# A weight ring with four slots instead of five, one more chunk kept resident, and value rows stored group by group

## The chip, the core and the metric

The kernel runs on one core of a Trainium2 chip. The metric is device microseconds (us) of one execution. Three runs of the kernel before took 1798.37, 1800.26 and 1802.88 us; the median is 1800.26 us.

## What is computed

The program computes two independent parts from the reference and writes them side by side.

```python
a = _A_ref(q, k, v, shift_k, ssm_k, ssm_D)   # short filter over k, times v, long convolution by FFT, times q
for s in range(n_seg):                        # B: 64 segments of 32 tokens, each behind the one before
    h = concatenate([mem, x[s]])              # 8 memory rows and 32 tokens, 1024 wide
    q, k, v = h @ Wq, h @ Wk, h @ Wv          # 32 heads of 128
    p = softmax(mask(q @ k.T * scale))
    o = (p @ v) @ Wo                          # 4096 -> 1024
    mem = o[:8]                               # memory of the next segment
    outs.append(o[8:])
return concatenate([a, b], axis=-1)
```

Part B is a recurrence: segment s+1 needs the first eight output rows of segment s. Its four weights hold 64 chunks of 128x2048 bf16 (512 KB each, 32 MB in all), more than fits on the chip, and all 64 are needed in every segment.

## The kernel before

**Stages.** Part A (L53 to L420) runs first, with dense work for part B filled into it: the keys and queries of 8 of each segment's 32 tokens (`dense`, L618) go to the DRAM tensor `REC`, and their value rows (L756 to L770) to `VBD`. After that the loop over segments (L920) holds all that is serial. In it the token matrix of 32 columns (8 memory rows and 24 tokens) goes through the projections in `Proj` (L933), and the 8 other tokens join from `REC` and `VBD`.

**Chunks.** `ORDER` (L26) lists the 64 chunks in the order of use in a segment as (matrix, chunk, group): 0 to 7 K and 8 to 15 Q in a mixed order, both of group 0 up to place 15; 16 to 23 K and 24 to 31 Q of group 1; 32 to 39 V of group 0 and 40 to 47 V of group 1; 48 to 63 the output weights, in the order `O_ORDER`. `STREAM` (L29) names the places that are not resident. There are 16; the two places 56 and 57 are loaded in segment 0 only and then kept in PSUM (`keep`, L821), so 14 chunks are streamed in each later segment: places 0, 6, 13, 19, 24, 29, 35, 40, 45, 51, 52, 54, 58 and 63. Of place 52 (`PART`) a quarter is resident, so its load has 384 KB. The other 48 chunks are resident, in tiles Wmid, Wres, Wmore, Wlate, pw and Wring.

**The ring.** Streamed chunks are first copied to the DRAM tensor `WS`. `fetch` (L715) takes the next chunk of the list `loads` and the slot that came free first, and issues the load on SyncE's queue (SP). `done` (L862) runs after the last matmul of a chunk: it gives its slot back and calls `fetch` once. With five slots (`free = [4, 5, 0, 1, 3]`, L708), a load is thus issued when the streamed chunk five places ahead of it in the stream has been used, and it has from then until its own use to land. Nothing else moves a load ahead. SP issues in program order, so an issue that waits holds up those behind it. The order of the matmuls is written out by hand (L1055 to L1125); a scheduler orders the work only ahead of the loop.

**Output weights.** In the loop the chunk at place 51 (output pair 3) is used in both column halves one after the other, ahead of the second attention; places 52 to 55 come next, then 58, and place 63 (pair 14) is the last of `LAST` in the first column half and the first in the second (L1115).

**GpSimd's queue (POOL)** issues in each segment, in this order: the two output stores (L1127), the load of the value rows `VBs` (L925), two copies into KT (L929), and the load of the next segment's token matrix `rec` from `REC` (192 KB, L882), which waits for the last V matmul.

**Slots that become resident.** Slots wring2 and wring3 serve as staging tiles (`pair`, `X_sb`, `xt`) ahead of the loop. In segment 0, wring3 becomes the fifth ring slot, and wring2 takes a resident chunk (L869) once the sixth streamed chunk is done. `late` lists the resident chunks that are loaded last; `place_late` takes them from its head.

**Value rows.** `VBD` has the layout [segment, token, c, i, (group, 128)]. The store of one group (L768) writes rows of 256 bytes, and the load of a segment (L925) reads both groups as rows of 512 bytes in one DMA.

Of the kernel before, what the change touches and what calls it, by code (L numbers as in the profile page):

```python
# [9 lines left out]
BF = mybir.dt.bfloat16  # L10
# [15 lines left out]
ORDER = [(0, kc, 0) for kc in (0, 1, 4, 5)] + [(1, kc, 0) for kc in (0, 1)] + [(0, kc, 0) for kc in (2, 3, 6, 7)] + \  # L26
    [(1, kc, 0) for kc in range(2, 8)] + [(m, kc, 1) for m in (0, 1) for kc in range(8)] + \
    [(2, kc, g) for g in range(2) for kc in range(8)] + [(3, hp, 0) for hp in O_ORDER]
STREAM = (0, 6, 13, 19, 24, 29, 35, 40, 45, 51, 52, 54, 56, 57, 58, 63)  # L29
N2, N3 = 12, 19  # L30
WO_COPY = 29
Q_LOAD = (10, 13, 16, 19)
X_LOAD = 1
STAGE3 = 34
LATE_RING = 5
RING = 5

PITCH = 2048
SCRATCH = 1024
# [383 lines left out]
def b_kernel(ctx: ExitStack, tc, x, mem0, Wq, Wk, Wv, Wo, outb, n_seg, run_a):  # L423
    nc = tc.nc
# [12 lines left out]
    streamed = set()  # L437
    for i in STREAM:
        streamed.add(order[i])
# [6 lines left out]
    late = [ch for ch in resident if ch not in placed]  # L446
# [15 lines left out]
    dram = ctx.enter_context(tc.tile_pool(name="b_dram", bufs=1, space=DRAM))  # L462

    REC = dram.tile([128, n_seg, 768], BF, name="REC")
    VBD = dram.tile([n_seg, 8, 4, 4, 256], BF, name="VBD")
    WS = dram.tile([len(ring_order), 128, PITCH], BF, name="WS")
    res = {}

# [10 lines left out]
    base = ctx.enter_context(tc.tile_pool(name="b0_base", bufs=1, side="right", reuse_waits="tile"))  # L479
# [3 lines left out]
    def xbt(kc):  # L483
        return XBT[kc // 4][:, kc % 4]
# [3 lines left out]
    def pair():  # L488
        turns["pair"] ^= 1
        return base.tile([128, 2048], BF, tag=f"wring{2 + turns['pair']}", name="pair")  # L490

    def slot16(shape, dt, name):
        turns["stage"] ^= 1
        return base.tile(shape, dt, tag=f"stage{turns['stage']}", name=name)
# [3 lines left out]
    def pw(k=None):  # L498
        if k is None:
            k = pw_next[0] % 8  # L500
            pw_next[0] += 1
        return pring.tile([128, 2048], BF, tag=f"pw{k}", name="pw")
# [63 lines left out]
    def group(m, g, temps={}, which=range(8), ws=None, eng=nc.sync, held=False):  # L566
        ws = ws or [None] * 8
        for kc in which:
            ch = (m, kc, g)
            if ch in res:  # L570
                got.append(eng.dma_start(res[ch], dram_chunk(ch)))
                ws[kc] = res[ch]
            else:
                t = temps[ch]() if ch in temps else pw()
                got.append(eng.dma_start(t[:], dram_chunk(ch)))
                if ch in streamed:
                    copies.append((stream_src(ch), t[:]))
                ws[kc] = t[:]
        while copies and not held:
            copied.append(nc.gpsimd.dma_start(*copies.pop(0)))  # L580
        return ws
# [28 lines left out]
    def evac(dst, src):  # L610
        flip[0] += 1
        if flip[0] % 3 and units[0] < STAGE3:
            nc.scalar.copy(dst, src)
        else:
            nc.vector.tensor_copy(dst, src)
# [35 lines left out]
    def store():  # L651
        if stores:
            nc.scalar.dma_start(*stores.pop(0))
# [40 lines left out]
    def more(i):  # L694
        return wres3.tile([128, 2048], BF, tag=f"Wmore{i}", name="Wmore")
# [5 lines left out]
    order_s = [ch for ch in order if ch in streamed]  # L701
    kept = {KEPT_A: "A", KEPT_B: "B"}
    at_hand = {}
# [1 line left out]
             if s == 0 and ch not in v_temp[2:] or s > 0 and ch not in kept]  # L705
    live = {}
    now = [0]
    free = [4, 5, 0, 1, 3]  # L708

    def slot():  # L710
        k = free.pop(0)
# [3 lines left out]
    def fetch():  # L715
        if loads:
            s, ch = loads.pop(0)
            live[s, ch] = k, t = slot()
            if ch in kept:
                nc.sync.dma_start(dst_view(t[:], ch), dram_chunk(ch))  # L720
            elif ch == PART:
                nc.sync.dma_start(t[:, 512:2048], stream_src(ch)[:, 512:2048])
            else:
                nc.sync.dma_start(t[:], stream_src(ch))

    def place(ch, ap):
        res[ch] = ap
        nc.sync.dma_start(dst_view(ap, ch), dram_chunk(ch))

    def place_late(n, tile_of):  # L730
        chs = [late.pop(0) for _ in range(n)]
        t = tile_of()
        for i, ch in enumerate(chs):
            place(ch, t[:, 2048 * i:2048 * i + 2048])
# [4 lines left out]
    with c0p:  # L739
        temps = dict(zip(v_temp, homes_v))  # L740
        wv = [group(2, 0, temps), None]
        for _ in rest:
            store()
        wv[1] = group(2, 1, temps)
        for i, ch in enumerate(v_temp):
            if i >= 2:
                home = (lambda i=i: more(i)) if i < len(v_temp) - 2 else (lambda k=i - len(v_temp) + 4: pw(k))
                at_hand[ch] = (wv[ch[2]][ch[1]], home)
        while stores:
            store()  # L750
        with tc.issue_after(got[-1].ins):
            for _ in range(2):
                fetch()
        n_k = len(own[0, 0])
        late = late[n_k:-2] + late[4:n_k] + late[:4] + late[-2:]
        for g in range(2):  # L756
            ws = wv[g]
            if g == 0:
                vsts = slot16([128, 4, 4, 512], BF, "vst")
            for tb in range(4):  # L760
                vst = vsts[:, tb] if g == 0 else pair()[:].rearrange("p (c w) -> p c w", c=4)
                for c in range(4):
                    ps = ps0.tile([128, 512], F32, tag="ps0", name="vb_ps")
                    for kc in range(8):
                        v_last = nc.tensor.matmul(ps[:], lhsT=xbt(kc)[:, 16 * tb:16 * tb + 16, :].rearrange("p s t -> p (s t)"),  # L765
                                                  rhs=ws[kc][:, c * 512:(c + 1) * 512], start=(kc == 0), stop=(kc == 7))
                    evac(vst[:, c, :], ps[:])
                nc.scalar.dma_start(  # L768
                    VBD[16 * tb:16 * tb + 16, :, :, :, g * 128:(g + 1) * 128].rearrange("s t c i e -> (s t) (c i) e"),
                    vst.rearrange("p c (i e) -> p (c i) e", i=4))  # L770
            if g == 0:
                with tc.issue_after(got[-1].ins):
                    place_late(4, stage_home)
                    for i in [*range(len(v_temp) - 2, n_more), *range(len(v_temp) - 2)]:
                        place_late(1, lambda: more(i))
                    place_late(1, lambda: pw(2))
                    place_late(4, stage_home)
        assert len(late) == len(at_hand) + 1

    one = ctx.enter_context(tc.tile_pool(name="b_one", bufs=1, side="right", reuse_waits="tile"))  # L780
    two = ctx.enter_context(tc.tile_pool(name="b_two", bufs=2, side="right", reuse_waits="tile"))
# [39 lines left out]
    def keep(ch):  # L821
        t = live[0, ch][1]
        if kept[ch] == "A":
            w = t[:].bitcast(I32).rearrange("p (hh dh f x) -> p hh f dh x", hh=2, dh=2, f=2)
            for q in range(4):
                bits(OTi[:, q, 160:416].rearrange("p (dh x) -> p dh x", dh=2), w[:, q // 2, q % 2])
        else:
            w = t[:].bitcast(I32)
            for q in range(4):
                for home, at in B_homes[q]:  # L830
                    n = home.shape[1] * (home.shape[2] if len(home.shape) == 3 else 1)
                    if len(home.shape) == 3 and n > 128:
                        for dh, o in enumerate(quarter_cols(q)):
                            bits(home[:, 2 * dh:2 * dh + 2, :], w[:, o // 2:o // 2 + 128].rearrange("p (b x) -> p b x", b=2))
                        continue
                    for dh, o in enumerate(quarter_cols(q)):
                        lo, hi = max(at, 128 * dh), min(at + n, 128 * dh + 128)
                        if lo < hi:
                            src = w[:, o // 2 + lo - 128 * dh:o // 2 + hi - 128 * dh]
                            bits(home if len(home.shape) == 3 else home[:, lo - at:hi - at], like(src, home))  # L840
# [21 lines left out]
    def done(ch):  # L862
        if now[0] == 0 and ch in at_hand:
            place_late(1, at_hand[ch][1])
        elif ch in streamed and (now[0] == 0 or ch not in kept):
            if now[0] == 0 and ch in kept:
                keep(ch)
            free.append(live.pop((now[0], ch))[0])
            if now[0] == 0 and ch == order_s[LATE_RING]:  # L869
                place_late(1, lambda: base.tile([128, 2048], BF, tag="wring2", name="Wring"))  # L870
            fetch()

    part = one.tile([128, 512], BF, name="part")
# [28 lines left out]
    with tc.manual_schedule():  # L902
        for _ in range(RING - 2):
            fetch()
# [15 lines left out]
        for s in range(n_seg):  # L920
# [1 line left out]
            last = s + 1 == n_seg  # L922
            hT, KBs, QBs = pend.pop(s)
            VBs = one.tile([128, 2, 128], BF, tag="VBs", name="VBs")
            nc.gpsimd.dma_start(VBs[:].rearrange("p g e -> p (g e)"), VBD[s].rearrange("t c i w -> (c i) t w"))  # L925

            def keys(g):
                KT = one.tile([128, 4, 4, 40], BF, tag="KT", name="KT")
# [271 lines left out]
```

## Time and profile before

| | |
|---|---|
| median of three runs | 1800.26 us |
| profiled execution, its own time | 1800.37 us |
| its span, first to last instruction | 1798.6 us |
| mean granted TensorE clock | 0.982 |
| first matmul of segment 0 / 1 / 63 | 440.33 / 471.52 / 1773.14 us |
| TensorE (PE) busy in 471.5 to 1791.5 us | 1297.27 of 1320 us |
| DMA share in the same stretch | 0.98, at 361 GB/s |
| DMA share in 364 to 438.7 us (value rows) | 0.99, at 307 GB/s |

Times in rows are us from the start of the span. In a timeline row the first number is the start, the second the duration of the whole row; several like instructions are merged ("x8"), and the bracket tells how long the engine sat idle before and who released it. A DMA has its issue on a queue ("SPq", "POOLq") and a landing, when its last byte has arrived; "to landing" counts from the start of the issue.

### The profile page before, as it was taken

The numbers are of one execution on the slowest core, as the hardware profiler recorded it, in microseconds if no ns is written. First come the engines' busy times: TensorE is split into PE (matmuls) and PEld (weight loads), VectorE is DVE, ScalarE is ACT, GpSimd is POOL, SyncE is SP. The second block draws the span as 40 slices with busy tenths as digits, with TensorE's granted clock in tenths as the row PEclk, the third lists the DMA queues.
The fourth block names the chain that finished last, engine by engine and source line by source line (L and its number), as shares of the span: only waits on it lengthen the run. The fifth ranks groups of instructions, "written<-read, shape, count | busy, mean of one in ns | idle before, by whom it ended". The sixth has DMA issues, their size and how long they took to land.

```text
span 1798.6 us, 70857 instructions
## 1 busy us (share of the span) xinstructions
PE 1690.5 (94%) x30744; PEld 995.1 (55%) x30776; DVE 1037.2 (58%) x3429; ACT 658.8 (37%) x1157; POOL 265.7 (15%) x499
## 2 busy tenths in 40 slices
PE   6988997697899999999999999999999999999998
PEld 2443323243566666666666666666666666666665
DVE  9926875432455555555555555555555555656555
ACT  6954651000233333333333333333333333333333
POOL 4102341100111111111111111111111111111111
PEclk9989998899899999999999999999999999999999
DMA  9989987999999999999999999999999999999998
GB/s 342 365 315 288 311 280 256 328 309 307 330 369 362 365 358 354 354 362 374 357 359 356 364 357 356 368 359 371 361 361 359 363 358 367 374 361 361 363 362 298
DMA packets 233069, 623.31 MB, mean 347 GB/s; under 512 B 72802, under 2 KB 72946, under 8 KB 232756
## 3 DMA queue, kind: packets, MB, share of 16 engines
q1 hardware_dynamic: 160948, 550.58, 82.8%
q0 software_dynamic: 17056, 45.13, 7.2%
q10 hardware_dynamic: 54752, 23.07, 4.8%
q8 instruction: 241, 3.95, 0.9%
q14 instruction: 72, 0.59, 0.1%
HBM read 563.63 MB, written 57.67 MB: 345 GB/s over the span
## 4 chain that ended last, share of the span: by engine, by line
PE 73%; DMA 13%; DVE 6%; ACT 5%; issue 3%; ACTq 1%; POOL 0%; SPq 0%; POOLq 0%; DVEq 0%
PE acc L945 32%; PE yacc L1036 21%; DMA wring<-WS 8%; PE kb_ps L624 5%; PE vb_ps L765 2%; PE tps L964 2%; ACT OT L1026 2%; PE tps L887 2%; DVE E L981 1%; DVE mx L979 1%; ACT s_sb L249 1%; DMA REC<-stage 1%; PE s_ps L247 1%; DMA VBD<-pair 1%; PE ks_ps L285 1%
## 5 line engine op out<-in xcount | busy, mean ns | idle before, releaser
L1036 PEld LDWEIGHTS <-OT 128*64 128x64 bf16 x8255 | 441.3, 110 | 52.8 <-ACT OT L1026 37.0
L945 PEld LDWEIGHTS <-rec 128*32 128x32 bf16 x12288 | 287.3, 96 | 277.2 <-DVE rec L898 41.2
L954 ACT CAST qkv_sb<-acc 128x512 bf16<-128x512 f32 x384 | 224.7, 585 | 519.1 <-PE acc L945 513.5
L945 PE MATMUL acc<-Wres,rec 128*32 128x512 bf16 x3328 | 239.5, 381 | 1.0 <-issue 0.9
L945 PE MATMUL acc<-wring,rec 128*32 128x512 bf16 x2300 | 227.9, 381 | 11.0 <-DMA wring<-WS 8.9
L1036 PE MATMUL yacc<-Wmore,OT 128*64 128x256 bf16 (+1 forms) x2560 | 221.2, 275 | 0.1
L945 PE MATMUL acc<-Wmid,rec 128*32 128x512 bf16 x3072 | 211.4, 379 | 0.9 <-issue 0.9
L1036 PE MATMUL yacc<-wring,OT 128*64 128x256 bf16 x2448 | 197.0, 274 | 6.2 <-DMA wring<-WS 3.2
L945 PE MATMUL acc<-pw,rec 128*32 128x512 bf16 x1796 | 144.4, 380 | 2.3 <-issue 2.2
L797 DVE TENSOR_SCALAR quarter<-OTp 128x256 int32<-128x256 int32 x252 | 99.5, 415 | 76.3 <-ACT OT L1026 76.3
L1125 ACT CAST Y<-yacc 128x256 bf16<-128x256 f32 x128 | 47.6, 372 | 257.8 <-DVE quarter_b L797 171.0
L1026 ACT CAST OT<-OTp 128x640 bf16<-128x640 f32 x128 | 87.4, 683 | 139.5 <-PE OTp L1018 139.4
L1127 POOL DMA_DIRECT2D out_dram<-Y x128 | 63.6, 502 | 485.0 <-ACT Y L1125 484.9
L945 PE MATMUL acc<-Wlate,rec 128*32 128x512 bf16 x1536 | 116.5, 379 | 0.0
L1064 DVE COPY KT<-tps 128x512 bf16<-128x512 bf16 x64 | 27.2, 425 | 153.8 <-PE tps L887 153.8
L898 DVE CAST rec<-tps 128x32 bf16<-128x32 f32 x128 | 24.5, 191 | 157.6 <-PE tps L896 153.6
L979 DVE TENSOR_REDUCE mx<-SB 128x8 f32<-128x320 f32 x128 | 62.9, 491 | 72.7 <-PE SB L973 72.7
L882 POOL DMA_DIRECT2D rec<-REC x64 | 36.2, 566 | 449.8 <-PE acc L945 433.7
L984 ACT ACTIVATE E<-E 128x320 f32<-128x320 f32 x128 | 60.1, 469 | 77.4 <-DVE E L981 77.3
L1036 PE MATMUL yacc<-Wlate,OT 128*64 128x256 bf16 x1024 | 78.9, 276 | 5.7
L624 PE MATMUL kb_ps<-XBT,pw 128*128 128x512 bf16 x314 | 81.6, 398 | 2.2 <-DMA pw<-in_B_Wk_dram 1.1
L929 POOL COPY KT<-rec 128x128 bf16<-128x128 bf16 x128 | 38.2, 299 | 263.2 <-PE SB L973 258.8
(222 smaller groups left out, 2630.6 us busy)
## 6 DMA issues: line engine op xcount, KB each, us to landing
wring<-WS SPq DMA_DIRECT2D x831, 512.0 KB, 6.1
wring<-WS SPq DMA_DIRECT2D x64, 384.0 KB, 5.4
rec<-REC POOLq DMA_DIRECT2D x64, 192.0 KB, 5.6
SK<-s_sb SPq DMA_DIRECT2D x16, 512.0 KB, 5.7
SU<-s_sb SPq DMA_DIRECT2D x16, 512.0 KB, 5.7
Kg<-SK SPq DMA_DIRECT2D x32, 256.0 KB, 4.3
Ug<-SU SPq DMA_DIRECT2D x32, 256.0 KB, 5.8
REC<-stage ACTq DMA_DIRECT2D x16, 512.0 KB, 13.0
```

The source lines that it names most:

```text
L624: nc.tensor.matmul(ps[:], lhsT=ws[kc][:, hl * 128:(hl + 1) * 128], rhs=xbt(kc).rearrange("p s t -> p (s t)"), start=(kc == 0), stop=(kc == 7))
L797: nc.vector.tensor_scalar(out=dst, in0=src, scalar1=0, scalar2=None, op0=ALU.bitwise_or)
L882: nc.gpsimd.dma_start(rec[:], REC[:, s, :])
L929: nc.gpsimd.tensor_copy(KT[:, :, :, 32:40], KBs[:, 128 * g:128 * g + 128].rearrange("p (c i t) -> p i c t", c=4, i=4))
L945: nc.tensor.matmul(self.acc[32 * c:32 * c + 32, :], lhsT=hT[:, ch[1], :], rhs=w[:, 512 * c:512 * c + 512], start=(ch == chs[0]), stop=(ch ...
L954: nc.scalar.copy(sb[:], self.acc[:])
L979: nc.vector.tensor_reduce(out=mx[:], in_=S, op=ALU.max, axis=AX.X)
L984: nc.scalar.activation(E[:], E[:], ACT.Exp, scale=scale)
L1026: nc.scalar.copy(OT[:], o_view)
L1036: nc.tensor.matmul(yacc[f][64 * dh:64 * dh + m, x - o:y - o], lhsT=lhsT, rhs=r, start=(h == (0, 2 * FIRST[-1])[f] and x == o), stop=stop, ...
L1125: nc.scalar.copy(Y[:, 256 * f:256 * f + 256], yacc[f][:, 0:256])
L1127: nc.gpsimd.dma_start(bass.AP(outb.tensor, outb.offset + SEG * s * 2048 + 512 * dh, [[2048, 32], [1, 512]]), Y[64 * dh + NM:64 * dh + 40, :])
```

## The change

```diff
-STREAM = (0, 6, 13, 19, 24, 29, 35, 40, 45, 51, 52, 54, 56, 57, 58, 63)
+STREAM = (0, 6, 13, 19, 26, 32, 38, 44, 51, 52, 55, 56, 57, 58, 63)
...
-LATE_RING = 5
-RING = 5
+LATE_RING = (5, 6)
+RING = 4
...
-    VBD = dram.tile([n_seg, 8, 4, 4, 256], BF, name="VBD")
+    VBD = dram.tile([2, n_seg, 8, 16, 128], BF, name="VBD")
...
-    free = [4, 5, 0, 1, 3]
+    free = [4, 5, 0, 1]
...
-        late = late[n_k:-2] + late[4:n_k] + late[:4] + late[-2:]
+        late = late[n_k:-3] + late[4:n_k] + late[:4] + late[-3:]
...
                 nc.scalar.dma_start(
-                    VBD[16 * tb:16 * tb + 16, :, :, :, g * 128:(g + 1) * 128].rearrange("s t c i e -> (s t) (c i) e"),
-                    vst.rearrange("p c (i e) -> p (c i) e", i=4))
+                    VBD[g, 16 * tb:16 * tb + 16].rearrange("s t h e -> (s t) (h e)"), vst.rearrange("p c w -> p (c w)"))
...
-            if now[0] == 0 and ch == order_s[LATE_RING]:
-                place_late(1, lambda: base.tile([128, 2048], BF, tag="wring2", name="Wring"))
+            if now[0] == 0 and ch in (order_s[i] for i in LATE_RING):
+                k = 2 + (ch == order_s[LATE_RING[1]])
+                place_late(1, lambda: base.tile([128, 2048], BF, tag=f"wring{k}", name="Wring"))
...
-            nc.gpsimd.dma_start(VBs[:].rearrange("p g e -> p (g e)"), VBD[s].rearrange("t c i w -> (c i) t w"))
+            for g in range(2):
+                nc.gpsimd.dma_start(VBs[:, g, :], VBD[g, s].rearrange("t h e -> h t e"))
```

Slot wring3 leaves the ring and takes a resident chunk in segment 0, as wring2 does, after the seventh streamed chunk. The ring has four slots, 49 chunks are resident, and a segment streams 13: places 0, 6, 13, 19, 26, 32, 38, 44, 51, 52, 55, 58 and 63. In `VBD` the two groups lie apart: a store writes one row of 4096 bytes for each partition, and a segment's value rows come in two DMAs with rows of 256 bytes.

More of the change, by code (lines that the diff above doesn't have):

```diff
@@ L777, in b_kernel @@
                     place_late(4, stage_home)
-        assert len(late) == len(at_hand) + 1
+        assert len(late) == len(at_hand) + 2
     one = ctx.enter_context(tc.tile_pool(name="b_one", bufs=1, side="right", reuse_waits="tile"))
```

## The prediction

> **What bounds the kernel now.** I read the stages first (busy times by stretch), then the chain that ended last, then single segments in the timeline, then the landings of single loads.
>
> The loop over segments takes 471.5 to 1791.5 us of a span of 1798.6. By stretch, value-row stage first, then the loop:
>
> ```profile
> 364.00:438.70 74.70, 62.37 (x277) 27.70 (x280) 24.00 (x35) 0.00 (x0) 4.10 (x8) 0.95 0.99 307
> 471.50:1791.50 1320.00, 1297.27 (x28490) 824.72 (x28490) 752.14 (x2830) 474.92 (x881) 168.70 (x377) 1.00 0.98 361
> ```
>
> The first figure after the stretch's length is PE busy, the last two are DMA share and GB/s. In the loop PE is busy 98% and the DMA engines 98%: both are nearly full. In the value-row stage PE is not (62.37 of 74.70 us), the DMA engines are.
>
> In the chain, in order of time, some segments are pure PE:
>
> ```profile
> 1518.25 4.49 PE yacc L1036 x80
> ...
> 1538.78 4.49 PE yacc L1036 x80
> ...
> 1559.31 4.49 PE yacc L1036 x80
> ```
>
> From one such row to the next is 20.53 us: the length of a segment in which nothing is waited for. The mean is (1773.14 - 471.52) / 62 = 20.99 us, from the starts of segments 1 and 63. So 0.46 us a segment, 29 us in 63 segments, is all that better loading could take from the loop. The waits tell what part of it is loads:
>
> ```profile
> PE acc L945 <- DMA wring<-WS: 8.9, 20, 1.1
> PE acc L945 <- issue: 4.5, 12, 0.9
> ```
>
> Ahead of the loop, two stalls come from the stores of value rows, as DVE waits for a staging tile whose store has not landed (7.03 + 2.20 us):
>
> ```profile
> 424.69 0.59 PE L765 MATMUL vb_ps<-pw,XBT 128*128 128x512 bf16 x1 [7.03 <-DVE pair L615]
> 435.25 0.38 PE L765 MATMUL vb_ps<-pw,XBT 128*128 128x512 bf16 x1 [2.20 <-DVE pair L615]
> ```
>
> **The change part by part.**
>
> *Value-row stores.* Eight stores of 512 KB change from 256-byte rows to 4096-byte rows. Now and beside it a ring load of the same size in 4096-byte rows:
>
> ```profile
> wring<-WS SPq DMA_DIRECT2D x831, 512.0 KB, 6.1
> VBD<-vst ACTq DMA_DIRECT2D x4, 512.0 KB, 15.1
> VBD<-pair ACTq DMA_DIRECT2D x4, 512.0 KB, 9.7
> ```
>
> The last number is us to landing. At 6.1 us a staging tile is free before its next use, two token blocks on (32 matmuls of 0.219 us, 7 us each), so both stalls go: 9.2 us. What is late next there is nothing that I see: the DMA engines fall idle after 434 us. The ends are 0 (another wait takes over) and 16 us; I take 9.2.
>
> *Segment 0* lasts 31.19 us (440.33 to 471.52), 10.7 over the floor, from loads that queue at its output weights. It gets one more resident load, two ring loads less in flight, and four streamed output chunks in a row (places 55 to 58). One load no longer waits on SP until the last value matmul (pw, issued at 437.39; its tile will be free a group earlier). I take 3 us gained, between -3 and 7.
>
> *Ahead of that* a copy to `WS` goes, and the scheduler shuffles some matmuls of part A's last stage with equal counts; 0, within 3 us either way.
>
> *Value-row loads.* POOL issues one more DMA of 0.53 us a segment (row VBs<-VBD). Behind it stands the first KT copy, now at 1210.95 us in one segment, whose reader starts at 1214.91: 3.4 us of cover are left. The second group lands about 1.93 + 1.07 + 5.6 us into the segment (issue and landing of today's rows); its readers come at 11.4 us: hidden. If that cover were gone, each us costs 63.
>
> *One chunk less, one slot less.* Traffic falls by 0.52 MB of some 7.5 MB a segment, 7%. That would ease the 0.46 us. But with four slots a load is issued after the use of the chunk four places ahead, not five. I took a segment without waits (start 1209.04) and read when each place is used. Rows of it:
>
> ```profile
> 1222.67 0.60 PE L1036 MATMUL yacc<-wring,OT 128*64 128x256 bf16 x8
> ...
> 1227.76 0.60 PE L1036 MATMUL yacc<-wring,OT 128*64 128x256 bf16 x8
> ```
>
> These are place 51 and place 63; SP issues the load after place 51 at 1223.31. The new places start, into the segment, at 0, 1.41, 2.93, 4.50, 6.48 (26), 8.21 (32), 9.94 (38), 11.80 (44), 13.63 (51), 14.72 (52), 16.43 (55), 17.09 (58) and 18.73 (63), next segment 20.53. An issue starts 0.44 us after a K, Q or V chunk starts and 0.64 after an output chunk. From issue to need, four places on, this leaves, in us: 4.85 for place 58, **4.46 for place 63**, 5.2 and 4.9 for the next segment's first two, 5.7 or more for all others. Today, with five slots, the shortest is 6.1.
>
> Place 63's load is issued at 14.27. Today a load is issued at that very point, for the next segment's place 0, and the trace tells how long it takes (three segments without waits, one of them the one above):
>
> ```profile
> L724 SPq DMA_DIRECT2D wring<-WS x1: 320/320/320, 1223.3 to 1223.3; - x1
> ...
> DMA to landing us min/median/max: 5.9/5.9/5.9
> ```
> ```profile
> L724 SPq DMA_DIRECT2D wring<-WS x1: 320/320/320, 1537.4 to 1537.4; - x1
> ...
> DMA to landing us min/median/max: 5.3/5.3/5.3
> ```
> ```profile
> L724 SPq DMA_DIRECT2D wring<-WS x1: 319/319/319, 611.2 to 611.2; - x1
> ...
> DMA to landing us min/median/max: 5.7/5.7/5.7
> ```
>
> Over the 22 undisturbed segments in which a landing is told the mean is 5.67 us (4.8 to 6.8). It is long although the load ahead was issued 1.8 us earlier, since the 192 KB of `rec` go out just before it (POOL, 1222.48). In the new kernel the load ahead is issued 2.0 us earlier, and `rec` at the same point, so I take 5.67. PE starts 0.04 us after a landing. Each segment then stalls 5.67 + 0.04 - 4.46 = 1.25 us at place 63. The ends are 0 (the shortest landing told of a ring load, 4.3 us, in the view of tile wring) and 1.7 (the page's median, 6.1).
>
> That stall moves the later issues only from place 63 on, so the next segment's first places gain 1.25 us of slack and need no wait of their own; a short wait at place 58 shifts place 63 as well and adds nothing.
>
> *Sum.* Stalls at place 63: 63 x 1.25 = +79. Of the 29 us of today's excess I let 17 go (load waits at the segment's start) and keep 12 (issue waits). Value rows -9, segment 0 -3. Together +79 - 17 - 9 - 3 = +50 us on the profiled execution's 1800.4 (1798.6 of span and 1.8 around it), which is the median of the runs (1800.3): **1850 us**.
>
> *A rule against this.* The Trainium skill (DMA: Bandwidth & Descriptors, section "Anatomy of one DMA — SWDGE (gpsimd) path") fits a DMA by "dma_µs ≈ 2.0 + bytes / 436e3"; for 512 KB that is 3.2 us, an estimate by that page, and place 63 would not stall. By that rule the time would be that of the first rival. The trace disagrees: no ring load in the loop lands within 4.3 us.
>
> **The rivals.**
>
> *No stall, faster.* With 7% less traffic the load for place 63 finds idle engines and lands in 4.3 us, as the quickest do now. Then only gains remain: -17 - 9 - 3 gives 1771. For it: the fewest DMAs are in flight around the middle of a segment. Against it: the 5.7 us are measured behind a load that itself landed early, so the queue is not what makes them; `rec` is. The turning point is a landing of 4.42 us.
>
> *Half a stall, no change.* `rec` is served sooner because less stands before it, and the load lands in 4.9 us: 63 x 0.45 = 28, less 29: 1800.
>
> *Late everywhere.* The loads do not get quicker on average and every landing stays at 6.1 us: place 63 stalls 1.7 us, nothing of the 29 us goes: +107 - 12 gives 1895. Against it: four loads cannot queue as deep as five.
>
> **How the numbers follow.** The forecast with stalls of 0.9 to 1.5 us gives 1828 to 1866. Chances: forecast 0.72, no stall 0.14, half a stall 0.09, late everywhere 0.05. The range is 1800 to 1870: it holds the forecast and the third case, and leaves out the other two. A measurement here tells 0.3% (5.4 us) from no change; faster by more 0.16 (the no-stall case and the lower edge of the third), within 0.06, slower by more 0.78 (the forecast, the last case and a little of the third).
>
> **What would show it.** Right: the first row of place 63 (last `wring` x8 row of a segment) waits about 1.2 us for a DMA in nearly every segment, segments last 21.8 to 22.0 us, `PE yacc <- DMA wring<-WS` sums to 60 us or more while `PE acc <- DMA wring<-WS` falls, DMA share in the loop falls to about 0.9, and no row shows vb_ps waiting for DVE pair. Wrong: segments of 20.6 us without that wait (first rival), or a landing of `rec` well under today's 5.6 us.

## The result and the profile after

The changed kernel takes 1855.42 us (median of four runs, 1853.29 to 1867.88) where the kernel before takes 1799.32 us beside it: a ratio of 1.032 with a 95% interval of 1.029 to 1.036. It is slower by about 56 us. The profiled execution took 1853.57 us with a span of 1851.8 us.

Ends of the stages in both traces tell where the 53.2 us of span came from. The loop's first matmul stands at 436.56 us (before: 440.33), segment 0 lasts 25.47 us (31.19), and the mean of the 62 segments after it is 22.01 us (20.99). So 3.8 and 5.7 us were gained up to segment 1, and 62 x 1.012 = 62.7 us were lost in the loop.

The same two stretches as before, value-row stage first, then the loop (PE busy comes behind the length; DMA share and GB/s are last):

```profile
362.00:434.90 72.90, 61.68 (x276) 27.17 (x275) 23.34 (x34) 0.00 (x0) 4.08 (x8) 0.95 0.91 319
462.03:1826.40 1364.37, 1288.92 (x28088) 816.14 (x28086) 743.83 (x2790) 467.13 (x868) 200.77 (x434) 1.00 0.93 322
```

In the loop PE is now busy 94% instead of 98% and the DMA engines 93% at 322 GB/s instead of 98% at 361: neither is full any more. Something that is neither work on PE nor bytes sets the pace. The waits of PE in 450 to 1845 us name it (us in total, times, longest):

```profile
PE yacc L1037 <- DMA wring<-WS: 47.5, 64, 2.1
PE acc L946 <- DMA wring<-WS: 17.9, 31, 1.8
...
PE acc L946 <- issue: 1.4, 2, 0.9
```

Before, the first of these rows was 3.2 us and the second 8.9. The chain of work that ended last shows it segment by segment. Where it had rows of pure PE from one output projection to the next, it now goes through one load in each segment:

```profile
1511.02 1.30 PE yacc L1037 x20
1512.34 5.41 DMA wring<-WS
1517.80 1.37 PE yacc L1037 x22
...
1532.58 1.30 PE yacc L1037 x20
1533.89 6.45 DMA wring<-WS
1540.39 1.37 PE yacc L1037 x22
```

The load is issued at 1512.34 (0.64 us after place 51 starts at 1511.70), takes 5.41 us, and PE goes on at once. That is place 63, as the timeline of the output chunks from `wring` shows:

```profile
1511.70 0.60 PE L1037 MATMUL yacc<-wring,OT 128*64 128x256 bf16 x8
...
1515.16 0.60 PE L1037 MATMUL yacc<-wring,OT 128*64 128x256 bf16 x8
1517.80 0.63 PE L1037 MATMUL yacc<-wring,OT 128*64 128x256 bf16 x8 [0.83 <-DMA wring<-WS]
```

0.84 us before that load POOL had issued `rec`:

```profile
1511.50 0.56 POOL L882 DMA_DIRECT2D rec<-REC  x1 [6.76 <-PE acc L946]
```

To see what every place loses, I compared each segment's matmuls, position by position, with the median of undisturbed segments of the kernel before (20.50 us on this scale). Mean excess in us a segment:

| | place 63 | place 58 | next segment's place 0 | place 6 | other loads | all loads | rest |
|---|---|---|---|---|---|---|---|
| before | 0.00 | 0.00 | 0.07 | 0.06 | 0.09 | 0.22 | 0.28 |
| after | 0.87 | 0.09 | 0.19 | 0.10 | 0.11 | 1.36 | 0.15 |

Place 63 waits over 0.06 us in 61 of 62 segments.

In the value-row stage one of the two stalls is still there:

```profile
422.95 1.86 PE L765 MATMUL vb_ps<-Wres,XBT 128*128 128x512 bf16 x4 [7.21 <-DVE pair L615]
```

Page, landings (KB each, us to landing):

```profile
wring<-WS SPq DMA_DIRECT2D x767, 512.0 KB, 5.5
wring<-WS SPq DMA_DIRECT2D x64, 384.0 KB, 4.6
rec<-REC POOLq DMA_DIRECT2D x64, 192.0 KB, 5.0
```

### The profile page after: what moved, and what is told of

Its sections match the earlier page's. It is cut to its first block, busy times and chain, and to the rows that moved or that the text cites. A ratio compares the mean times of both kernels' runs of the same rounds, so it can differ in the third digit from the quotient of the medians.

```text
span 1851.8 us, 70765 instructions
## 1 busy us (share of the span) xinstructions
PE 1700.0 (92%) x30776; PEld 992.7 (54%) x30776; DVE 1039.2 (56%) x3429; ACT 658.0 (36%) x1157; POOL 300.2 (16%) x562
## 4 chain that ended last, share of the span: by engine, by line
PE 61%; DMA 29%; ACT 4%; DVE 3%; issue 1%; ACTq 1%; POOL 0%; POOLq 0%; SPq 0%; DVEq 0%
PE acc L946 33%; DMA wring<-WS 23%; PE yacc L1037 11%; PE kb_ps L624 5%; PE tps L965 2%; ACT OT L1027 2%; DMA REC<-stage 2%; PE tps L887 2%; ACT s_sb L249 1%; PE OTp L1015 1%; PE s_ps L247 1%; ACTq L653 1%; DMA Wmore<-in_B_Wo_dram 1%; PE ks_ps L285 1%; PE vb_ps L765 1%
## 5 line engine op out<-in xcount | busy, mean ns | idle before, releaser
L946 PE MATMUL acc<-Wres,rec 128*32 128x512 bf16 x3328 | 248.7, 380 | 1.4 <-issue 1.4
L1037 PE MATMUL yacc<-wring,OT 128*64 128x256 bf16 (+1 forms) x2448 | 196.1, 273 | 50.3 <-DMA wring<-WS 47.5
L946 PE MATMUL acc<-wring,rec 128*32 128x512 bf16 x2044 | 200.7, 382 | 19.9 <-DMA wring<-WS 17.9
L1037 PE MATMUL yacc<-Wmore,OT 128*64 128x256 bf16 x2560 | 196.9, 274 | 0.0
L946 PE MATMUL acc<-Wlate,rec 128*32 128x512 bf16 x1792 | 141.5, 379 | 0.0
L1037 PE MATMUL yacc<-Wring,OT 128*64 128x256 bf16 (+1 forms) x1024 | 97.4, 273 | 0.0
L926 POOL DMA_DIRECT2D VBs<-VBD x128 | 68.6, 538 | 47.3 <-DMA VBD<-pair 23.4
```

The costliest lines, as they stand in the source:

```text
L926: nc.gpsimd.dma_start(VBs[:, g, :], VBD[g, s].rearrange("t h e -> h t e"))
L946: nc.tensor.matmul(self.acc[32 * c:32 * c + 32, :], lhsT=hT[:, ch[1], :], rhs=w[:, 512 * c:512 * c + 512], start=(ch == chs[0]), stop=(ch ...
L1037: nc.tensor.matmul(yacc[f][64 * dh:64 * dh + m, x - o:y - o], lhsT=lhsT, rhs=r, start=(h == (0, 2 * FIRST[-1])[f] and x == o), stop=stop, ...
```

## The experiments

**Theory**: in the loop a place stalls when the time from its load's issue to its use (its window) is shorter than the landing; the fourth slot, not the places, took the time; `rec`, sent just ahead, lengthens place 63's landing. **Rivals**: the places or the value rows took the time; or four slots are short everywhere, so that a stall only moves.

### A fifth slot given back

```diff
-RING = 4
+RING = 5
-LATE_RING = (5, 6)
+LATE_RING = (5,)
...
+                res[late.pop(0)] = res[3, 15, 0]
```

The 49th resident chunk has no tile then, so the output matmuls of pair 11 use another pair's weights.

> The changed kernel with a fifth ring slot again and its 13 loads and places as they are. The slot is won by leaving one output chunk out: pair 11 reads pair 15's weights, so the output is not the reference's. Theory (a load has only the time from the use of its slot to its own use; with four slots place 63 has 4.46 us and its load takes 5.4): every window grows to 5.9 us or more, the waits at place 63 go, segments last 20.6 to 20.8 us and the time is 1765 to 1785 us. Rival (the new value-row loads, two a segment in rows of 256 bytes, slow the loop): the time stays above 1830 us.

Measured: 1789.57 us, ratio to the kernel before 0.993 (0.991 to 0.996); segments of 20.93 us. Waits of PE in 462 to 1800 us, here and in the changed kernel:

```profile
PE acc L946 <- DMA wring<-WS: 5.4, 11, 0.8
PE acc L946 <- issue: 2.9, 7, 0.6
```
```profile
PE yacc L1037 <- DMA wring<-WS: 45.4, 61, 2.1
PE acc L946 <- DMA wring<-WS: 17.9, 31, 1.8
```

The output chunks' waits are gone from the list. The fifth slot is worth 66 us (1855.42 - 1789.57); one load less a segment, with the new value rows, gains 12 us on the 1801.20 of the kernel before beside it. The time is 5 us above the theory's range, and the segments are 0.13 us longer than it said: of the 0.42 us that a segment lasts over the undisturbed one, about 0.32 are not loads.

### A slot taken from the kernel before

```diff
-RING = 5
+RING = 4
-    free = [4, 5, 0, 1, 3]
+    free = [4, 5, 0, 1]
```

> The kernel before with the fifth slot left unused, 14 loads and its own places. Windows shrink to 4.46 us for place 63, 4.6 for place 58, 5.2 for place 0. Theory of the window: place 63 waits at least as long as in the changed kernel (0.9 us a segment and more, since 8% more traffic is under way): 1850 to 1890 us. Rival (what made the changed kernel slower is its new places, not the slots): 1800 to 1815 us.

Measured: 1913.51 us, ratio 1.063 (1.061 to 1.066), segments of 22.86 us. Waits of PE in 462 to 1800 us:

```profile
PE yacc L1036 <- DMA wring<-WS: 60.4, 89, 2.5
PE acc L945 <- DMA wring<-WS: 30.8, 59, 1.6
```

With the places of before, a missing slot costs 112 us (the kernel before took 1801.20 beside it), more than the theory's 50 to 90. So the slot is the cause, and the change's shorter list of loads had already taken back part of its price (the even places below show how much).

### The value rows alone, and undone

In the kernel before, the change's `VBD`, stores and loads; then, in the changed kernel, those of before. First:

```diff
-    VBD = dram.tile([n_seg, 8, 4, 4, 256], BF, name="VBD")
+    VBD = dram.tile([2, n_seg, 8, 16, 128], BF, name="VBD")
```

> The kernel before with the new layout of the value rows alone, five slots and 14 loads as before. Theory: the loop is as before (20.9 to 21.1 us a segment), the stage of value rows gains 0 to 6 us: 1790 to 1800 us. Rival (two loads of 256-byte rows a segment slow the loop): 1815 us or more.

Measured: 1798.05 us, ratio 0.998 (0.996 to 1.000). The loop begins 2.6 us sooner, segment 0 is 5.4 us shorter (25.82), and the loop's segments are 0.1 us longer (21.09). Executions of the kernel before lie between 1793.7 and 1808.8 us, 0.24 us a segment apart, so the last part tells nothing.

The second, with the opposite edit:

> The changed kernel with the value rows' layout in DRAM, their stores and their load as before. Theory by the prediction's step (both waits for staging tiles go, 9.2 us): 1862 to 1868. Rival, by the run of the new layout alone in the kernel before (1798.05 against 1801.2, 3 us of the span of it before the loop, and some of it given back in the loop by the second load): 1855 to 1860.

Measured: 1863.85 us, 8.4 above the changed kernel's 1855.42. The two were not run side by side: against the kernel before beside each, the ratios are 1.036 (1.032 to 1.039) and 1.032 (1.029 to 1.036), and the intervals overlap. So the traces have to tell. They differ by 11.2 us of span: the loop begins 0.8 us later with the old rows, segment 0 lasts 30.49 us instead of 25.47, and the loop's segments are 0.1 us longer (22.10 against 22.01), the other way round than in the pair above. Segment 0 by stretch (length, PE busy; at the end granted clock, DMA share, GB/s), with the old layout and with the new:

```profile
437.38:467.87 30.49, 23.86 (x452) 15.27 (x453) 12.95 (x49) 8.35 (x14) 0.85 (x2) 0.89 0.89 317
```
```profile
436.56:462.03 25.47, 21.32 (x452) 13.04 (x452) 12.95 (x49) 8.34 (x14) 0.86 (x2) 1.00 0.98 354
```

Half of the 5.0 us is idle time, half is PE busy for longer with the same 452 matmuls, at a lower clock. The timeline of the output chunks shows the idle time, again old and new:

```profile
459.10 0.63 PE L1037 MATMUL yacc<-wring,OT 128*64 128x256 bf16 x8 [3.03 <-DMA wring<-in_B_Wo_dram]
461.81 1.06 PE L1037 MATMUL yacc<-wring,OT 128*64 128x256 bf16 x8 [2.08 <-DMA wring<-in_B_Wo_dram]
```
```profile
457.95 0.63 PE L1037 MATMUL yacc<-wring,OT 128*64 128x256 bf16 x8 [2.59 <-DMA wring<-in_B_Wo_dram]
459.23 0.63 PE L1037 MATMUL yacc<-wring,OT 128*64 128x256 bf16 x8 [0.66 <-DMA wring<-WS]
```

The same eight matmuls take 1.06 us in the second row instead of 0.63: the clock has fallen. What stands beside the loads is the last store, on queue q10 (packets, MB, share of the engines' time), old and new:

```profile
q10 hardware_dynamic: 2064, 0.52, 7.7%
```
```profile
q10 hardware_dynamic: 144, 0.52, 5.2%
```

So the new layout does help, and most clearly at segment 0's output weights and in the clock behind them; up to the loop it gave 0.8 and 2.6 us. A third pair, the last two kernels below, has 26.02 us for segment 0 with the new rows and 28.69 with the old. By medians the layout is worth 3 to 8 us. That the 2064 packets are what makes those loads late fits the pairs, but was not tried by itself, and the new rows alone do not keep segment 0 short: it lasts 29.13 us in the changed kernel with `rec` in two parts.

### Other places with four slots

The places of before without 54:

```diff
-STREAM = (0, 6, 13, 19, 26, 32, 38, 44, 51, 52, 55, 56, 57, 58, 63)
+STREAM = (0, 6, 13, 19, 24, 29, 35, 40, 45, 51, 52, 56, 57, 58, 63)
```

> Four slots and 13 loads as in the changed kernel, but the places of before without place 54: 0, 6, 13, 19, 24, 29, 35, 40, 45, 51, 52, 58, 63. The shortest window from issue to need is 5.4 us (for place 52), and place 63 has 6.3. Theory of the window: no wait at place 63, short waits spread over the places, segments of 20.8 to 21.1 us, time 1780 to 1805 us. Rival (four slots are too few wherever the places lie, as fewer loads are under way): 1830 us or more.

Measured: 1825.15 us, ratio 1.014 (1.012 to 1.016). It lies between the two: 30 us better than the changed kernel, 36 worse than with five slots. Against the same places with 54 as a fourteenth load (1913.51), one load less gains 88 us. So with four slots the number of loads and the places count too: of the 66 us between four and five slots, the change's choice of places made 30. Then a list that gives place 63 a window of 6.05 us:

```diff
-STREAM = (0, 6, 13, 19, 26, 32, 38, 44, 51, 52, 55, 56, 57, 58, 63)
+STREAM = (0, 6, 13, 19, 25, 31, 37, 42, 46, 52, 55, 56, 57, 58, 63)
```

> The changed kernel with four ring slots and 13 loads, but other places: 0, 6, 13, 19, 25, 31, 37, 42, 46, 52, 55, 56, 57, 58, 63. Place 63's load is now issued after the use of place 46, not 51, 1.6 us sooner, so its window from issue to need is about 6.05 us instead of 4.46; place 58's is about 5.4 instead of 4.85, those of the next segment's first two stay 5.2 and 4.9, no other is under 5.6. Theory (the window against the landing decides, place by place): the 0.87 us a segment at place 63 go, and nearly nothing comes in their place, since the loads landed in 5.4 to 6.0 us: segments of 21.0 to 21.3 us, 1795 to 1815 us. Rival (four slots cannot keep the queue fed, whatever the places; the stall moves to another place): 1835 or more, with the same sum of load waits.

Measured: 1831.18 us, ratio 1.017 (1.014 to 1.020), segments of 21.66 us. That is 16 us above the theory's range and 4 below the rival's. Waits of PE in 462 to 1800 us:

```profile
PE acc L946 <- DMA wring<-WS: 42.5, 72, 1.6
PE yacc L1037 <- DMA wring<-WS: 5.7, 9, 0.9
```

Against the changed kernel (45.4 and 17.9 us) the two rows have changed places. By position, place 63 fell from 0.87 to 0.09 us, as its window of 6.05 us lets one expect; but place 6 of the next segment, with a window of 4.9 us and a median landing of 5.37, rose from 0.10 to 0.36, and all loads together only from 1.36 down to 1.07 us. In the even list it is 0.99. So each place follows its own window, and yet the rival is nearly right about the sum: most of the stall moved. My expectation had taken the windows of 4.9 and 5.2 us for sufficient while naming landings of 5.4 to 6.0: the stall at place 63 had covered them.

### `rec` in two parts

```diff
-        rec = one.tile([128, 768], BF, tag="rec", name="rec")
-        nc.gpsimd.dma_start(rec[:], REC[:, s, :])
+        recx = one.tile([128, 256], BF, tag="recx", name="recx")
+        nc.gpsimd.dma_start(recx[:], REC[:, s, 0:256])
...
+    def load_kq(s):
+        rec = one.tile([128, 512], BF, tag="rec", name="rec")
+        nc.gpsimd.dma_start(rec[:], REC[:, s, 256:768])
...
             scores(1, QT1, KT1)
+            if not last:
+                load_kq(s + 1)
```

> The changed kernel, but the 192 KB of the next segment's rec are loaded in two parts: 128 KB (keys and queries of the last tokens) soon after the second group's scores, 64 KB (hT) at the old point, just ahead of the load for place 63. Theory (what goes out just ahead of that load lengthens its landing): 128 KB at the loop's 320 GB/s are 0.4 us, so the landing of place 63's load falls from 5.36 to about 4.95 us after its issue starts, its stall from 0.87 to about 0.45 us a segment, and the time by some 27 us, to 1820 to 1835. Rival (the depth of loads in flight makes the landing, rec does not matter): 1849 to 1861, the stall at place 63 stays at 0.8 or more.

Measured: 1842.62 us, ratio 1.023 (1.020 to 1.026): 13 us gained, between the two. The profile is of the slowest of its five executions (1850.85 us, the others up to 1842.82), so the figures below tell less than the 13 us: segments of 21.88 us, and a segment 0 of 29.13. Waits of PE in 462 to 1800 us:

```profile
PE yacc L1045 <- DMA wring<-WS: 32.6, 55, 1.8
PE acc L954 <- DMA wring<-WS: 21.5, 38, 2.0
```

By position, place 63 fell from 0.87 to 0.40 us (expected: 0.45), its median landing from 5.36 to 5.08 us. But the 128 KB now go out at about 11.4 us into the segment, ahead of place 58's load, whose landing rose from 4.48 to 4.97 us and whose stall rose from 0.09 to 0.34. A wait at place 58 also shifts place 63's use, so part of the fall at 63 is that shift. All loads together fell only from 1.36 to 1.23 us. The lengthening follows the bytes: what `rec` does to the load behind it is shown, and it is a part of the stall, not all of it.

With five slots there is room for it. The split with the new value rows in the kernel before:

> The kernel before (five slots, 14 loads) with the change's layout of the value rows, and rec loaded in two parts as in the run above. In that kernel the load issued just behind rec is the one for the next segment's place 0, with a window of 6.3 us. Theory: waits for loads are about 0.2 us a segment there, so at most 12 us are to be had, and 2 to 10 come: 1788 to 1796. Rival (POOL's additional issue of about 0.5 us a segment delays the first copy of keys behind it): 1803 or more.

Measured: 1787.00 us, ratio 0.992 (0.989 to 0.994), better than the kernel before and than the changed one, and 1 us better than the theory's range. Segments last 20.92 us. Its waits in 462 to 1800 us, and those without the split:

```profile
PE acc L953 <- issue: 3.3, 8, 0.7
PE yacc L1044 <- DMA wring<-WS: 2.4, 4, 1.2
PE acc L953 <- DMA wring<-WS: 2.0, 6, 0.7
```
```profile
PE acc L945 <- DMA wring<-WS: 8.4, 15, 1.2
PE acc L945 <- issue: 4.7, 8, 1.1
PE yacc L1036 <- DMA wring<-WS: 1.6, 2, 1.0
```

The split alone in the kernel before:

> The kernel before with rec loaded in two parts and nothing else. Theory (shorter landings of the load behind rec, whatever the layout of the value rows): the 11 us by which the split improved the kernel with the new layout come here too, 1787 to 1794. Rival (the split gained only because the new layout's second load had cost something): 1797 to 1803.

Measured: 1792.59 us, ratio 0.994 (0.992 to 0.997). The split gains by itself, as the theory had it; with the value rows' 0.998 the product is 0.992, what both together gave.

## Why the prediction came out right, step by step

**Total.** Forecast 1850, measured 1855.42; the cause, the lost slot, is shown in both directions (66 us with 13 loads, 112 with 14); of the 66, 30 hang on where the 13 places lie. That the loop's sum was met so closely (62 us forecast, 63 measured) is luck: the stall at place 63 was forecast 25 us too large, and the waits at other places were forecast to shrink by 17 us and grew by 17.

**The signs that were named.** Right: the wait at place 63 in nearly every segment, the length of a segment (22.01 us) and the DMA share (0.93). Not so: `PE yacc <- DMA wring<-WS` came to 47.5 us, not 60; `PE acc <- DMA wring<-WS` rose; a row of vb_ps still waits for DVE pair. And `rec` landed in 5.0 us instead of 5.6, which the prediction had put among the signs of being wrong: that part of its argument for a landing of 5.67 us did not hold.

**The stall at place 63** (63 x 1.25 = 79 us). Mechanism right, size too large: 0.87 us, 54 us. The window was read well. The landing was the mis-sized term: median 5.36 us against 5.67, and 5.36 + 0.04 - 4.46 = 0.94. `rec`, which goes out ahead of it, landed in 5.0 us instead of 5.6; by the run with `rec` in two parts the two go together.

**"The next segment's first places ... need no wait of their own."** Wrong: place 0 waits 0.19 us and place 6 0.10 us a segment, and `PE acc <- DMA wring<-WS` rose from 8.9 to 17.9 us instead of falling. Place 0's load is issued at 15.5 us and its landing, which I did not work out, is 5.90 us in the median and 6.75 in one case of ten, against 5.2 + 0.87 us. I compared windows with a typical landing, and the spread decides near the edge. Place 58 (window 4.85, median landing 4.48) is the same: 0.09 us, up to 1.18 in single segments.

**"Of the 29 us I let 17 go."** Wrong in kind: load waits other than place 63's rose by 0.49 - 0.22 = 0.27 us a segment (17 us) and the rest fell by 0.13 (8 us). Together with 54 us that is the measured 63; the forecast for the loop was 79 - 17 = 62.

**Value rows** (-9.2). Size near, place wrong. The wait of 2.20 us went, the one of 7.03 became 7.21. ACT's queue in 404 to 437 us shows that the store of the first `pair` tile was issued late, at 414.96 us, though DVE had filled the tile by 406.1:

```profile
408.36 0.33 ACTq L768 DMA_DIRECT2D VBD<-vst  x1
414.96 21.22 ACTq L768 DMA_DIRECT2D VBD<-pair  x4
```

From 408.69 to 414.96 us the queue issues nothing. I had counted the store from the filling of its tile. The chain of work that ended last names what it waited for:

```profile
402.31 12.57 DMA Wmore<-in_B_Wo_dram
...
414.90 0.02 ACTq L768
...
414.96 7.12 DMA VBD<-pair
```

That is the load of a resident output chunk into `Wmore`, which has nothing to do with the tile. In the trace the load and the store report their landing on the same semaphore (103), and the store is issued as soon as the load has landed; no run tries it without. What the layout is worth (3 to 8 us) came mostly in segment 0.

**Segment 0** (-3) became -5.7; by the run with the old rows 5.0 of it are the layout, so loads and slots by themselves gave little. The larger part of it, 3.6 us, is the clock: PE was busy 24.96 us in it before, at a mean clock of 0.84, and 21.32 after, at 1.00 (the row is shown above). Before:

```profile
440.33:471.52 31.19, 24.96 (x452) 16.40 (x453) 12.83 (x49) 8.34 (x14) 0.85 (x2) 0.84 0.94 346
```

Value rows, segment 0 and what lies ahead together were forecast at -12.2 and measured at -9.5 (3.8 + 5.7).

**The second load of value rows**, costed at nothing: no cost is seen. No row of PE waits for `VBs` among the rows of 0.2 us or more in the loop, and segments with the old single load are no shorter (22.10).

**Rivals.** "No stall" fell with the first profile: the landing would have had to be 4.42 us. The Trainium skill's fit (DMA: Bandwidth & Descriptors, "Anatomy of one DMA — SWDGE (gpsimd) path"), 3.2 us for this size, is under every ring load of the loop after, too; it is a fit for the GpSimd path, and these loads are issued on SP:

```profile
DMA to landing us min/median/max: 3.7/5.5/7.8
```

"Half a stall" had something right: `rec` was served sooner, and the load landed in 5.36 us, between its 4.9 and the forecast's 5.67. "Late everywhere" had the truer picture of the other places, if not the size: four slots leave no place much to spare. The mean time from issue to need is slots x 20.53 / loads less about 0.5 us to the issue, in us:

| | slots, loads | mean window | landing by the page | segment |
|---|---|---|---|---|
| a fifth slot given back | 5, 13 | 7.4 | 6.0 | 20.93 |
| before | 5, 14 | 6.8 | 6.1 | 20.99 |
| after | 4, 13 | 5.8 | 5.5 | 22.01 |
| even places | 4, 13 | 5.8 | 5.7 | 21.55 |
| before with four slots | 4, 14 | 5.4 | 5.7 | 22.86 |

With 0.3 us or less between the second column and the third a segment lasts 0.6 to 1.9 us longer than with 0.7 or more. Among the rows with four slots the margin does not order the segments (0.3 us and 22.01, 0.1 us and 21.55): there the places decide how it is shared out.

## What to carry to other kernels

Size a ring by its mean window, slots x period / loads, against the landing under load and its spread, before placing single loads; a margin of 0.3 us was not enough here, and with 0.7 a segment still waited 0.22 us for loads. Trading one slot for one resident chunk took 7% off the traffic and 15% off the windows. A wait that is removed at one place uncovers the windows behind it, so work out the next segment again without it; and a bulk load sent just ahead of the load with the least slack can be split and sent where slack is.

## What the runs showed of the hardware

A wait of PE can cost more than itself. In the value-row stage after the change, the clock fell within the wait of 7.21 us (415.74 to 422.95 us):

```profile
420.00:422.00 2.00, 0.00 (x0) 0.00 (x0) 0.00 (x0) 0.00 (x0) 0.00 (x0) 0.50 1.04 420
```

In segment 0 of the changed kernel with the old rows, with 3.03 and 2.08 us of idleness close together, the granted clock of the two stretches of 4 us from 460 us on was 0.55 and 0.60:

```profile
460.00:464.00 4.00, 1.99 (x18) 1.69 (x19) 2.75 (x10) 0.00 (x0) 0.00 (x0) 0.55 0.96 377
464.00:468.00 4.00, 4.00 (x50) 3.77 (x50) 0.19 (x1) 0.40 (x2) 0.00 (x0) 0.60 0.87 284
```

With the new rows, with waits of 2.59 and 0.66 us, it stayed at 1.00; with `rec` in two parts, waits of 1.61 and 2.01 us within 4.3 us (to 460.96) sufficed for 0.50:

```profile
462.00:464.00 2.00, 1.76 (x18) 1.75 (x19) 0.80 (x2) 0.00 (x0) 0.00 (x0) 0.50 0.63 227
```

The Trainium skill (TensorE: Matmul & The Clock Gate, section "Part 1: The HAM clock gate (the "warmup" mystery)") has the clock halved after an idle window of about 3.4 us; these rows agree, and add that two shorter waits close together do it too. The stalls of 0.9 us once in a segment of the loop did not: the clock is 1.00 there.

With fewer bytes in flight the landings shortened from 6.1 to 5.5 us (10%), and the loop's rate fell by 11% (361 to 322 GB/s), but the engines' busy share only by 5% (0.98 to 0.93): the share and the rate did not move together.
